# Row maxima of the values pinned behind the first two score maxima in a fused attention and MoE kernel

## Chip, cores and metric

The kernel runs on one core of one Trainium2 chip. The metric is the device time of one execution in microseconds (us). "Profile" and "trace" mean one execution recorded by the hardware profiler.

## What is computed

Two batches of eight heads, 768 positions, head size 64: attention in which a query sees only the keys of its own hash bucket (six sign bits of a projection), and then two dense layers over 1536 tokens.

```python
q_bits = (np.einsum('bhsd,dk->bhsk', q, proj) > 0)
mask = q_bucket[:, :, :, None] == k_bucket[:, :, None, :]
scores = np.where(mask, scale * np.matmul(q, k.transpose(0, 1, 3, 2)), -1000000000.0)
attn = np.exp(scores - np.max(scores, axis=-1, keepdims=True))
attn = attn / (np.sum(attn, axis=-1, keepdims=True) + 1e-09)
x = np.matmul(attn, v)          # then heads side by side: 1536 x 512
h = x @ w_in;  x = (h / (1 + exp(-h))) @ w_out
h = x @ w_in2; out = (h - tanh(h)) @ w_out2
```

## The kernel before

**Tiles.** A tile is 128 queries against the 768 keys of one head: 6 tiles a head, 48 a batch, numbered 0 to 95 here. For a tile `scores` (L243) makes four matmuls into PSUM tile `ps`. `soft_max` (L256, VectorE) copies them to `p` and takes their row maximum. `soft_exp` (L264, L265, ScalarE) takes the exponential. Then `p`, split into two float16 halves, is transposed into `pt`. Odd tiles of the first batch do that on TensorE (`turn_p`: L278, with L280 on ScalarE and L281 on VectorE). All others go through `soft_hi` (L290, ScalarE), `soft_lo` (L297, GpSimd) and a DMA transpose on SyncE's queue (L299). `pv` (L311 to L313) multiplies `pt` by the values; in the program it comes six tiles behind the scores.

**Hash bits.** `hash_mm(n)` (L172) runs once a head. VectorE turns its result into bits `hb` (L185), and two DMAs issued by ScalarE (L187, L188) copy them into the operands of the second half of the head's scores.

**Values.** `load_v` (L194) brings a batch's values into `vr` with three DMAs. `prep_vm` (L202, VectorE) takes the largest magnitude of each row, in six pieces of 128x512, into `vm`. `prep_v0` makes one scale `vsc` of them (L210 on VectorE, the matmul L212, L213 to L217 on VectorE). `prep_v2` splits the scaled values into `v16` (L232, ScalarE) and `v16l` (L233, VectorE), six pieces each; `pv` needs both. The second batch's `vr` lies in the same buffer as the first's, so its DMAs wait for the last L233 of the first batch.

**Stages.** The first batch's 48 tiles go with TensorE alone to themselves. From tile 33 on weights are loaded (L466) and split on VectorE (L507, L508, L510, L497), ScalarE (L498, L506) and GpSimd (L499). Thirteen steps pass without new scores between the batches. From tile 48 on scores have one `ps` buffer, not two, so a tile's scores wait for the maximum of the tile before. Groups of the first dense pass (L530, L554, twelve matmuls each) lie between the tiles of the second batch; the other passes follow after it.

**Order.** Every engine executes its own instructions strictly in a list order. The lists are made by a scheduler from the written program, from priorities and from its own estimate of time. `@early` (L92) raises the priority of what a function issues, so that the scheduler may place it ahead of older work. `tc.keep_in_program_order(...)` keeps an instruction in its place of the written order on its engine. In the loop over steps `prep_vm` is called behind `soft_exp` of a batch's first and second tile, three pieces each (L408).

Of the kernel before, what the change touches and what calls it, by code (L numbers as in the profile page):

```python
# [12 lines left out]
ALU = mybir.AluOpType  # L13
AXL = mybir.AxisListType
# [35 lines left out]
def lsh_attention_moe_kernel(  # L50
# [12 lines left out]
    nc = tc.nc  # L63
# [46 lines left out]
    def attention(pools, vraw, extra, xw):  # L110
# [9 lines left out]
        hlx, vmxs = {}, {}  # L120
# [70 lines left out]
        def load_v(b):  # L191
            vr = vraw.tile([128, NQ, DM], F32, tag="acc", name="vr")
            for t in range(0, NQ, 2):
                nc.sync.dma_start(out=vr[:, t:t + 2, :],  # L194
                                  in_=v[b, t * 128:(t + 2) * 128].rearrange("(t p) d -> p t d", p=128))
            return vr

        @early
        def prep_vm(b, vr, t):
            if t == 0:  # L200
                vmxs[b] = sm.tile([128, NQ], F32, tag="vm", name="vm")
            nc.vector.tensor_reduce(vmxs[b][:, t:t + 1], vr[:, t, :], axis=AXL.X, op=ALU.max,  # L202
                                    apply_absolute_value=True)

        @early
        def prep_v0(b, vr):
# [159 lines left out]
        vr = load_v(0)  # L366
# [8 lines left out]
        for s in range(B * (per + gap)):  # L375
# [18 lines left out]
            if i is not None:  # L394
                n, t = divmod(i, NQ)
# [9 lines left out]
            if i is not None:  # L405
                if i % per < 2:
                    for u in range(3):
                        prep_vm(n // H, vr, 3 * (i % per) + u)  # L408
                if i % per == 1:
                    prep_v0(n // H, vr)  # L410
                    prep_v1(n // H, vr)
                if 2 <= i % per < 4:
                    for u in range(3):
                        prep_v2(n // H, vr, 3 * (i % per - 2) + u)
                if prep[0] < NHEAD and prep[0] <= limit(n):
                    if prep[1] == 0:
                        split_a(prep[0])
                    elif prep[1] == 1:
                        split_b(prep[0])
                    prep[1] += 1  # L420
                    if prep[1] == 3:
                        prep[:] = [prep[0] + 1, 0]
                while nextr < NHEAD and nextr <= (limit(n) + 1 if n < H - 1 else n + (2 if t >= 3 else 1)):
                    load_qk(nextr)
                    nextr += 1
                if n + 1 < NHEAD:
                    if (n + 1) % H == 0 and t == 0:
                        vr = load_v((n + 1) // H)
# [304 lines left out]
```

## Time and profile before

| | |
|---|---|
| time, median of 3 runs | 792.09 us (791.6 to 792.28) |
| the profiled execution: its own time | 791.22 us |
| its span, first to last instruction | 789.4 us |
| TensorE busy (PE) | 733.6 us, 93% |
| VectorE (DVE) | 544.4 us, 69% |
| ScalarE (ACT) | 433.1 us, 55% |
| GpSimd (POOL) | 309.5 us, 39% |

The own time holds 1.8 us that lie around the span. PE's busy time is a sum over stages of very different kind; what an edit is worth is read from the stage in which it lies. PE in a row is TensorE's matmul, SPq and ACTq are the queues by which SyncE and ScalarE issue DMAs.

### The profile page before, as it was taken

Reading aid. Unit: us, or ns where it says so; the run is one execution under the profiler, and the core shown is the slowest. Engines: PE = TensorE matmul, PEld = TensorE weight load, DVE = VectorE, ACT = ScalarE, POOL = GpSimd, SP = SyncE. Lnnn points to the kernel's source line nnn. Section 1 sums busy time; section 2 is a strip of 40 time slices with the busy share of each in tenths; the row PEclk is TensorE's granted clock in tenths of the full one; section 3 lists DMA queues with packets and bytes.
Section 4 is the critical chain, followed back from the end, with each engine's and each line's share of the span. In section 5 each row is a group of like instructions: output and inputs, shape, how many; then the busy total and the mean of one; then the engine's idle time right before and its main releaser. Section 6 shows DMA issues by size and latency. Waiting matters only on the chain.

```text
span 789.4 us, 14334 instructions
## 1 busy us (share of the span) xinstructions
PE 733.6 (93%) x5492; PEld 700.0 (89%) x5492; DVE 544.4 (69%) x1029; ACT 433.1 (55%) x821; POOL 309.5 (39%) x214
## 2 busy tenths in 40 slices
PE   4778798789989899999999999999999999999998
PEld 3667677679978798899999999999999999999998
DVE  6968688798878778778542443998768576584342
ACT  4849788797788678667443441553524334242130
POOL 4536537466777667566455420222111110110000
PEclk8899899899999999999999999999999999999999
DMA  7695776969999899994333320323112121210102
GB/s 255 190 148 106 126 154 167 212 155 197 263 245 211 214 180 240 215 218 136 97 104 107 95 81 1 101 90 130 53 56 78 57 81 33 75 54 0 52 29 81
DMA packets 138879, 100.39 MB, mean 127 GB/s; under 512 B 115870, under 2 KB 118174, under 8 KB 138810
## 3 DMA queue, kind: packets, MB, share of 16 engines
q1 hardware_dynamic: 137712, 97.54, 50.6%
q10 hardware_dynamic: 1098, 1.94, 1.0%
q8 instruction: 43, 0.70, 0.3%
q14 instruction: 26, 0.21, 0.1%
HBM read 57.95 MB, written 11.53 MB: 88 GB/s over the span
## 4 chain that ended last, share of the span: by engine, by line
PE 55%; DMA 2%; ACT 1%; DVE 0%; issue 0%; POOL 0%; ACTq 0%; DVEq 0%
PE psm L554 28%; PE psm L530 26%; DMA pt<-hl 1%; DMA w<-wi 1%; PE ps L243 0%; ACT xh L577 0%; ACT p L265 0%; POOL hl L297 0%; PE pso L311 0%; POOL wl L485 0%; ACT wh L484 0%; ACT th L536 0%; PE pso L312 0%; PE pso L313 0%; ACT hl L290 0%
## 5 line engine op out<-in xcount | busy, mean ns | idle before, releaser
L499 POOL TENSOR_TENSOR wl<-wa,wh 128x512 fp32r<-128x512 f32 x64 | 83.8, 1309 | 244.3 <-ACT wh L498 244.3
L530 PE MATMUL psm<-xh,wh 128*128 128x384 f32 x512 | 173.2, 339 | 1.6 <-ACT wh L484 1.6
L554 PE MATMUL psm<-gh,wh 128*128 128x384 f32 x512 | 173.0, 338 | 0.6 <-ACT x L346 0.4
L554 PE MATMUL psm<-gl,wh 128*128 128x384 f32 x512 | 171.5, 335 | 0.0
L530 PE MATMUL psm<-xl,wh 128*128 128x384 f32 x512 | 171.4, 335 | 0.0
L530 PE MATMUL psm<-xh,wl 128*128 128x384 f32 x512 | 170.0, 335 | 0.0
L554 PE MATMUL psm<-gh,wl 128*128 128x384 f32 x512 | 169.4, 335 | 0.0
L297 POOL TENSOR_TENSOR hl<-p,hl 128x768 f16<-128x768 f32 x72 | 120.4, 1674 | 88.0 <-ACT hl L290 82.5
L256 DVE TENSOR_SCALAR_CACHE_REDUCE p<-ps 128x768 f32<-128x768 f32 x96 | 90.8, 952 | 29.7 <-PE ps L243 20.0
L530 PEld LDWEIGHTS psm<-xh,wh 128*128 128x128 f32 x512 | 96.5, 188 | 2.1 <-ACT wh L484 1.9
L243 PE MATMUL ps<-k,q 128*128 128x384 f32 x336 | 82.9, 372 | 15.9 <-DVE p L256 9.0
L554 PEld LDWEIGHTS psm<-gh,wh 128*128 128x128 f32 x512 | 96.3, 188 | 1.5 <-ACT x L346 0.6
L554 PEld LDWEIGHTS psm<-gl,wh 128*128 128x128 f32 x512 | 96.4, 188 | 0.0
L530 PEld LDWEIGHTS psm<-xl,wh 128*128 128x128 f32 x512 | 96.4, 188 | 0.0
L566 DVE TENSOR_TENSOR acc<-acc,psm 128x384 f32<-128x384 f32 x96 | 52.1, 551 | 63.5 <-PE psm L554 63.1
L530 PEld LDWEIGHTS psm<-xh,wl 128*128 128x128 f32 x512 | 95.9, 188 | 0.0
L554 PEld LDWEIGHTS psm<-gh,wl 128*128 128x128 f32 x512 | 95.8, 188 | 0.0
L542 DVE TENSOR_TENSOR gl<-psm,gh 128x384 fp32r<-128x384 f32 x128 | 70.6, 554 | 31.9 <-ACT gh L541 31.7
L265 ACT ACTIVATE p<-p,bi 128x768 f32<-128x768 f32 x96 | 89.0, 939 | 2.9
L541 ACT CAST gh<-psm 128x384 fp32r<-128x384 f32 x128 | 61.4, 480 | 50.5 <-DVE psm L540 35.1
L311 PE MATMUL pso<-v,pt 128*128 128x65 f16 x576 | 70.9, 200 | 15.4 <-DMA pt<-hl 15.3
L311 PEld LDWEIGHTS <-pt 128*128 128x128 f16 x576 | 55.3, 101 | 27.2 <-DMA pt<-hl 17.4
(90 smaller groups left out, 1267.2 us busy)
## 6 DMA issues: line engine op xcount, KB each, us to landing
w<-in_w_in_dram SPq DMA_DIRECT2D x32, 512.0 KB
w<-in_w_out_dram SPq DMA_DIRECT2D x32, 512.0 KB
r<-in_qkT_dram SPq DMA_DIRECT2D x15, 768.0 KB
wi<-wa SPq DMA_DIRECT2D x16, 256.0 KB
wo<-wa SPq DMA_DIRECT2D x16, 256.0 KB
w<-wi SPq DMA_DIRECT2D x16, 256.0 KB
w<-wo SPq DMA_DIRECT2D x16, 256.0 KB
vr<-in_v_dram SPq DMA_DIRECT2D x6, 512.0 KB
```

The costliest lines, as they stand in the source:

```text
L243: nc.tensor.matmul(out=ps[:, u, 0:HS], lhsT=a[:, t * 128:(t + 1) * 128], rhs=c[:, u * HS:(u + 1) * HS], start=(j == 0), stop=(j == 1))
L256: nc.vector.tensor_scalar(p.rearrange("p (c s) -> p c s", c=2), pss.pop(i)[:, :, 0:HS], FLOOR, None, op0=ALU.max, op1=ALU.max, accum_out=m)
L265: nc.scalar.activation(out=p, in_=p, func=ACTF.Exp, scale=0.125, bias=bi)
L297: nc.gpsimd.tensor_tensor(hl[:, 1, :], p, hl[:, 0, :], op=ALU.subtract)
L311: nc.tensor.matmul(out=o, lhsT=pt[:, kt, :], rhs=v16[:, kt, h, :], start=(kt == 0), stop=False)
L499: nc.gpsimd.tensor_tensor(ll, s, hh.bitcast(F32), op=ALU.subtract)
L530: nc.tensor.matmul(out=ps, lhsT=a[:, k, fs], rhs=b_[blk][:, k, :], start=(k == 0 and j == 0), stop=(k == KD - 1 and j == 2))
L541: nc.scalar.copy(gh[:, f, :], ps)
L542: nc.vector.tensor_tensor(gl[:, f, :], ps, gh[:, f, :].bitcast(F32), op=ALU.subtract)
L554: nc.tensor.matmul(out=ps, lhsT=a[:, f, ds], rhs=b_[:, f, :], start=(f == 0 and j == 0), stop=(f == F - 1 and j == 2))
L566: nc.vector.tensor_tensor(ac, ac, ps, op=ALU.add)
```

## The change

`prep_vm` loses `@early`, and its reduction is kept in program order.

```diff
-        @early
         def prep_vm(b, vr, t):
             if t == 0:
                 vmxs[b] = sm.tile([128, NQ], F32, tag="vm", name="vm")
-            nc.vector.tensor_reduce(vmxs[b][:, t:t + 1], vr[:, t, :], axis=AXL.X, op=ALU.max,
-                                    apply_absolute_value=True)
+            tc.keep_in_program_order(
+                nc.vector.tensor_reduce(vmxs[b][:, t:t + 1], vr[:, t, :], axis=AXL.X, op=ALU.max,
+                                        apply_absolute_value=True))
```

No instruction is added or removed in the computation; the scheduler's lists differ. VectorE's list at the start of the program (L179 and L181 write tile 0's hash bits, L202 are the row maxima, L256 the score maxima of tiles 0 to 3, L210 the first step to the scale):

```order
-L202 TENSOR_REDUCE vm<-vr 128x1 x2
 L179 TENSOR_SCALAR q_145<-psm,cst_sb 18x384
 L181 TENSOR_SCALAR k_147<-psm,cst_sb 18x384
-L202 TENSOR_REDUCE vm<-vr 128x1 x4
+L256 TENSOR_SCALAR p,mx<-ps 128x768
+L202 TENSOR_REDUCE vm<-vr 128x1 x3
+L256 TENSOR_SCALAR p,mx<-ps 128x768
+L202 TENSOR_REDUCE vm<-vr 128x1 x3
 L256 TENSOR_SCALAR p,mx<-ps 128x768 x2
 L210 TENSOR_REDUCE vmx<-vm 128x1
```

All six row maxima stood ahead of tile 0's score maximum; now three stand behind tile 0's and three behind tile 1's.

ScalarE's list somewhat later in the same opening (L187 and L188 are the two DMAs with head 1's hash bits, L232 the six pieces of `v16`, L280 the copies of tile 1's transposes):

```order
+L265 ACTIVATE p<-p,bi 128x768
+L187 DMA q_187<-hb 18x768
 L232 ACTIVATE v_221<-vr,vsc 128x8x64 x6
-L187 DMA q_187<-hb 18x768
+L280 CAST pt<-psm 128x384 x2
 L188 DMA k_189<-hb 18x768
```

The second DMA of the bits stood right behind the six pieces; now two copies more stand ahead of it, and the exponentials of tiles 4 and 5 (L265) stand ahead of the pieces, where there were those of tiles 0 to 3 alone.

TensorE's list in the first batch, near tile 27 (L172 with h and l makes the hash of head 5 in two groups of four, of which the second is shown here; L243 with 649 and 650 are scores of head 4, four matmuls a tile; L278 are transposes). Before:

```order
L243 MATMUL ps<-k_649,q_647 128x384 x2
L243 MATMUL ps<-k_650,q_648 128x384 x2
L172 MATMUL psm<-h_129,hw 82x384
L172 MATMUL psm<-l_130,hw 82x384 x2
L172 MATMUL psm<-h_129,hw 82x384
L278 MATMUL psm<-cst_sb,p 128x128 x3
```

And now:

```order
L172 MATMUL psm<-h_129,hw 82x384
L172 MATMUL psm<-l_130,hw 82x384 x2
L172 MATMUL psm<-h_129,hw 82x384
L243 MATMUL ps<-k_649,q_647 128x384 x2
L243 MATMUL ps<-k_650,q_648 128x384 x2
L243 MATMUL ps<-k_649,q_647 128x384 x2
L243 MATMUL ps<-k_650,q_648 128x384 x2
L278 MATMUL psm<-cst_sb,p 128x128 x9
L243 MATMUL ps<-k_649,q_647 128x384 x2
L243 MATMUL ps<-k_650,q_648 128x384 x2
```

Three tiles' scores that stood ahead of the end of this hash (the third is the one shown in the rows before) stand behind it now.

VectorE's list where the second batch begins. Before, from tile 48's score maximum (its batch's row maxima stand some forty tiles earlier in the list):

```order
L256 TENSOR_SCALAR p,mx<-ps 128x768
L281 TENSOR_TENSOR pt<-psm,pt 128x384 x2
L256 TENSOR_SCALAR p,mx<-ps 128x768
L319 TENSOR_SCALAR den<-pso,vsc 128x6
L320 RECIPROCAL den<-den 128x6
L329 TENSOR_TENSOR xt<-pso,den 128x6x64
L507 TENSOR_SCALAR cv<-cv 128x512
L256 TENSOR_SCALAR p,mx<-ps 128x768
L508 TENSOR_SCALAR cv<-cv 128x512
L213 TENSOR_REDUCE vmr<-psm 128x1
```

And now, from the same maximum:

```order
L256 TENSOR_SCALAR p,mx<-ps 128x768
L202 TENSOR_REDUCE vm<-vr 128x1 x3
L281 TENSOR_TENSOR pt<-psm,pt 128x384
L256 TENSOR_SCALAR p,mx<-ps 128x768
L507 TENSOR_SCALAR cv<-cv 128x512
L319 TENSOR_SCALAR den<-pso,vsc 128x6
L202 TENSOR_REDUCE vm<-vr 128x1 x3
L508 TENSOR_SCALAR cv<-cv 128x512
L320 RECIPROCAL den<-den 128x6
L256 TENSOR_SCALAR p,mx<-ps 128x768
L210 TENSOR_REDUCE vmx<-vm 128x1
L510 SCALAR_TENSOR_TENSOR cv<-w,cv 128x512
```

The six row maxima of the second batch, which stood near tiles 8 and 9 of the first, stand behind tiles 48 and 49. The last step to the scale (L217) stood between the maxima of tiles 51 and 52 and stands between those of 52 and 53 now.

## Rows read from the trace of the kernel before

**Rows 1.** Stages by windows: busy us of each engine, clock, DMA share, GB/s
```profile
0.00:46.00 46.00, 26.23 (x183) 21.94 (x184) 37.09 (x71) 30.00 (x51) 24.20 (x19) 0.89 0.79 214
46.00:134.00 88.00, 75.17 (x864) 64.73 (x861) 66.37 (x142) 68.68 (x136) 45.49 (x27) 0.92 0.66 132
...
152.00:182.00 30.00, 25.38 (x260) 23.55 (x259) 28.11 (x52) 25.99 (x49) 18.00 (x13) 0.95 0.68 173
182.00:362.00 180.00, 171.41 (x1584) 156.92 (x1582) 143.81 (x283) 135.98 (x243) 119.08 (x78) 0.99 1.02 218
362.00:789.40 427.40, 421.88 (x2433) 420.97 (x2432) 256.07 (x460) 160.08 (x323) 93.97 (x75) 1.00 0.22 70
```

**Rows 2.** Timeline of TensorE: start, us, work, idle before it and releaser
```profile
28.91 2.26 PE L243 MATMUL ps<-k,q 128*128 128x384 f32 x6 [3.27 <-DMA k<-hb]
...
45.47 0.20 PE L311 MATMUL pso<-v,pt 128*128 128x65 f16 x1 [3.43 <-DMA pt<-hl]
...
88.53 0.98 PE L243 MATMUL ps<-l,h 128*128 128x384 f32 x2 [3.45 <-DMA l<-hb]
```

**Rows 3.** What TensorE waited for, 134 to 400 us: total, times, longest
```profile
PE pso L311 <- DMA pt<-hl: 10.8, 7, 3.9
PE pso L312 <- DVE v16l L233: 3.6, 2, 2.2
```

**Rows 4.** Timeline of VectorE, opening
```profile
13.39 2.46 DVE L202 TENSOR_REDUCE vm<-vr 128x1 f32<-128x512 f32 x4
15.89 0.96 DVE L256 TENSOR_SCALAR_CACHE_REDUCE p<-ps 128x768 f32<-128x768 f32 x1
...
22.18 0.14 DVE L217 TENSOR_SCALAR vsc<-vmr 128x1 f32<-128x1 f32 x1
...
29.97 0.95 DVE L256 TENSOR_SCALAR_CACHE_REDUCE p<-ps 128x768 f32<-128x768 f32 x1
...
30.85 1.45 DVE L233 SCALAR_TENSOR_TENSOR v16l<-vr,vsc,v 128x512 f16<-128x512 f32 x1
```

**Rows 5.** ScalarE: the page's group of exponentials, then its timeline, opening
```profile
L265 ACT ACTIVATE p<-p,bi 128x768 f32<-128x768 f32 x96 | 89.0, 939 | 2.9
...
22.55 1.32 ACT L232 ACTIVATE v<-vr,vsc 128x512 f16<-128x512 f32 x2
...
24.89 0.74 ACTq L188 DMA_DIRECT2D k<-hb  x1
```

**Rows 6.** SyncE's queue: timeline in the opening, then the page's sizes of issues
```profile
32.32 1.41 SPq L194 DMA_DIRECT2D vr<-in_v_dram  x3
...
34.58 13.24 SPq L299 DMA_TRANSPOSE pt<-hl  x3
...
r<-in_qkT_dram SPq DMA_DIRECT2D x15, 768.0 KB
...
vr<-in_v_dram SPq DMA_DIRECT2D x6, 512.0 KB
```

**Rows 7.** Chain that ended last: one DMA transpose
```profile
322.84 5.53 DMA pt<-hl
```

**Rows 8.** Tiles vm and v16l on VectorE: ns min/median/max, starts
```profile
L202 DVE TENSOR_REDUCE vm<-vr x12: 675/676/687, 10.8 to 41.7; 128x1 f32<-128x512 f32 x12
L233 DVE SCALAR_TENSOR_TENSOR v16l<-vr,vsc,v x12: 740/776/2429, 23.3 to 176.6; 128x512 f16<-128x512 f32 x12
```

**Rows 9.** Timeline of VectorE where the second batch begins
```profile
152.27 0.95 DVE L256 TENSOR_SCALAR_CACHE_REDUCE p<-ps 128x768 f32<-128x768 f32 x1
...
164.22 0.15 DVE L217 TENSOR_SCALAR vsc<-vmr 128x1 f32<-128x1 f32 x1
...
172.02 2.43 DVE L233 SCALAR_TENSOR_TENSOR v16l<-vr,vsc,v 128x512 f16<-128x512 f32 x1
...
174.97 3.38 DVE L233 SCALAR_TENSOR_TENSOR v16l<-vr,vsc,v 128x512 f16<-128x512 f32 x2
```

**Rows 10.** Timeline of GpSimd, same place
```profile
171.83 2.07 POOL L159 TENSOR_TENSOR q<-r,q 64x768 fp32r<-64x768 f32 x1 [3.97 <-ACT q L151]
```

## Prediction

> **What bounds the kernel now.** I first cut the span into stages. In the windows [rows 1] read TensorE's busy time against the length of each. From 362 us on it is 421.9 of 427.4 us, from 182 to 362 us 171.4 of 180. Those stages end when TensorE has done its work, so whatever moves their beginning moves the end. Up to 46 us it is busy 26.2 of 46, and from 46 to 134 us 75.2 of 88: there TensorE stands because something else is late. The DMA share of 1.02 from 182 to 362 us says that the 16 DMA engines have work all that time too. An edit on VectorE counts by what it adds to or takes from TensorE's idle time before 362 us.
>
> So I read next, in TensorE's timeline, what ends its long waits [rows 2]. At 28.91 it has stood 3.27 us for head 1's hash bits (k<-hb). At 45.47 it has stood 3.43 us for the DMA transpose of tile 4. At 88.53 it has stood 3.45 us for head 5's hash bits. Where the second batch begins it stands 3.6 us in two pieces for `v16l` [rows 3]. The row maxima end none of these waits themselves. They are work in VectorE's list, and the question is what they push.
>
> **The opening.** Each row maximum takes 0.675 us [rows 8], 0.61 to 0.64 us from start to start (four in 2.46 us) [rows 4]. Before, two of them, from 10.8 on [rows 8], delay the second half of tile 0's bits by 1.3 us, and four more fill 13.39 to 15.85, so tile 0's maximum starts at 15.89. Take them away: the two operations on the bits end at about 12.1 instead of 13.4, I give the scores behind them 0.6 us, and tile 0's maximum starts at 12.7, 3.2 us earlier. That is the edit's gain, and it does not last. Tile 1's maximum waits for three row maxima: 12.7 + 0.9 + 1.9 = 15.5. Three more follow, and tiles 2 and 3 come at 18.2 and 19.1. In the new list tiles 4 and 5 come before the scale's steps (L213 on), so 18.2 + 4 x 0.9 = 21.8 is where these begin. They need 1.6 us up to 22.3 now; the new list puts a second eviction of hash bits (0.7 us) among them, and that one waits for hash matmuls which now stand behind the scores of tiles 4 and 5. The scale is ready at about 24.7 instead of 22.3.
>
> The loss grows on ScalarE. Its six pieces of `v16` began at 22.55, right behind the scale [rows 5]. In the new list five more items stand ahead of them (two copies for head 3, one half of tile 4, the exponentials of tiles 4 and 5), each at most as long as an exponential, 0.94 us [rows 5]; I count 0.85 each. What stands ahead of those five ends 0.8 us earlier by the opening above. So they begin at 22.55 - 0.8 + 4.25 = 26.0. The second hash DMA, issued at 24.89 and landed by 28.91, is behind two further copies of about 0.4 us: 24.9 + 3.45 + 0.7 = 29.0, landed at about 33. Tile 6's maximum, 29.97 now, comes at about 34.1, and behind it in VectorE's list are two pieces of `v16l` and tile 7's maximum (0.75, 0.9, 0.75), so the last L233 ends at 37.2 instead of 32.3. For that SyncE's queue waits: the second batch's `vr` is issued at 32.32 [rows 6], in its list ahead of tile 4's transpose, which is issued at 34.58 and lands at 45.47, 13.15 us behind `vr`'s issue. In the new list the 768 KB of `r` that stood between them go out earlier. One transpose alone takes 5.53 us [rows 7], which leaves 7.6 us for the 2304 KB ahead of it and 2.5 us for `r`, a third of them. Tile 4's transpose then lands at 37.2 + 13.15 - 2.5 = 47.9: **+2.4 us** at the point where, by both lists, TensorE has done the same work. What is queued behind is the whole of TensorE's list. Bounds: -2 (the `vr` DMAs no later and `r` out of the way) to +5 (the hash bits land at 36). The row maxima of the second batch no longer fill VectorE from 36 to 42 us; that saves TensorE nothing here, because the transpose of tile 4 lands later than they end.
>
> **The hash of head 5.** TensorE's new list has three tiles' scores behind this hash that stood ahead of its end. The 3.45 us wait at 88.53 then has twelve more matmuls beside it, of which two take 0.98 us there [rows 2], enough to cover it. But the bits' second DMA still waits on ScalarE behind a copy of transposes, which now stand behind two of those tiles. I take **-2 us**; bounds -3.4 (all of it) and 0.
>
> **The start of the second batch.** From tile 48's maximum at 152.27 to the end of the last `v16l` piece takes 26.1 us now [rows 9]. VectorE works in 28.1 of the 30 us around [rows 1], so there is little idle time in which six row maxima could hide. The new list adds between these two points six of them (3.7), L210 (0.15) and three steps of weight splitting (2.0), and leaves out two others (1.0): +4.8 us if the gaps stay. Two things counter it. The 1.9 us of gaps fill up. And the last three L233 took 2.43 and 3.38/2 us against 0.74 at best [rows 8, 9], while GpSimd subtracted operands of the next head [rows 10]; whether the later pieces meet that again the trace cannot tell. If none did, 4.0 us would be saved. So the last piece comes between 1.1 us earlier and 4.8 later. In TensorE's list one group of the dense pass (12 matmuls, 2.1 us) that lay ahead of the wait for it lies behind it now, which takes that cover away. Together -1.1 to +6.9; I take **+4**, nearer the upper end, because head 10's operands are prepared directly behind the scale in both lists and will meet these pieces again.
>
> The Trainium skill (page "SBUF — State Buffer", section "Who interferes with whom") says that a VectorE instruction with two SBUF inputs contends with a GpSimd instruction that reads SBUF, whichever comes first holding the shared ports to its end, and that a reduction does not. The trace agrees: L202 never leaves 675 to 687 ns, L233 ranges from 740 to 2429 [rows 8]. By that rule the moved row maxima cost their plain time anywhere, and each moved L233 may cost a whole GpSimd instruction; the third rival is that case.
>
> **After that.** From 182 to 362 us TensorE waits for transposes 6.9 us in all (10.8 [rows 3] less the 3.9 before). A later TensorE also shifts what feeds those DMAs, so I count no gain; bounds -4 to +3, because the lists there differ in many small places.
>
> **Sum.** +2.4 - 2 + 4 = +4.4 on the profiled execution's 791.2 us gives 795.6. The median of the runs is 0.9 above that execution, where it would be 796.5. I say **796**.
>
> **Rivals.**
> 1. *The gain stays and the losses are eaten.* Place: head 5's bits at 85 to 88.5 us. Its wait goes entirely (-3.4), while the lateness of 2.4 goes into the other waits between 46 and 134 us (12.8 us not busy [rows 1]) and the second batch's into the 6.9 us of waits for transposes. Time 791.2 - 3.4 = 788. For it: these waits exist. Against it: most are for things that TensorE's own work sets off. It decides if what is left of both losses is under 1.8 us. Chance 0.2.
> 2. *Nothing arrives at the end.* The DMA engines, busy all through 182 to 362 us [rows 1], set the pace of the second batch, and lateness of TensorE up to there is hidden behind them: 791 to 793. For it: the share of 1.02. Against it: TensorE is busy for 95% of that stage, which leaves 8.6 us to hide in. Chance 0.2.
> 3. *All six late pieces meet GpSimd.* 1.7 us each (2.43 - 0.74) makes 10.1 instead of 4.0 us, 6 us more: about 802. Chance 0.08.
>
> That the pin does nothing is excluded by VectorE's lists, in which all twelve reductions stand elsewhere. My forecast, a few us slower, has the rest, 0.52; its own range is 793.7 to 800.
>
> **Numbers.** 0.2% of 792 is 1.6 us, about what a measurement here can tell from no change. Slower: 0.52 + 0.08 = 0.6. Same 0.2, faster 0.2. The range 789.5 to 802 leaves out perhaps 0.12 below and 0.07 above.
>
> **What would show it.** Tile 0's maximum at 12 to 13 us, the scale at 24 to 25, k<-hb landing at 32 to 34, TensorE's wait for the first late transpose ending at 47 to 49. Head 5's wait of 1 to 2 us instead of 3.45. From tile 48's maximum to the last `v16l` piece 29 us or so, and TensorE waiting for `v16l` 6 us or more instead of 3.6. The end then follows the start of the dense passes unchanged. I would be wrong if the hash bits of head 1 landed by 30 us, if the pieces of `v16l` all took 0.75 us, or if scheduling differences between 182 and 362 us, which I have set to nothing, came to several us.

## Result and the profile after

The kernel became slower: a median of 799.46 us over four runs (797.97 to 802.77) against 791.85 us of the kernel before beside it; ratio 1.0111, 95% interval 1.0067 to 1.0156. The profiled execution took 797.97 us, its span 796.2.

The forecast of 796 named the right side and the size within 3.5 us. The trace shows that the time went elsewhere than I had said. These are the stages of the changed kernel by windows, as in [rows 1]:

```profile
0.00:46.00 46.00, 28.06 (x208) 23.26 (x209) 31.28 (x65) 30.96 (x53) 23.29 (x19) 0.89 0.71 214
46.00:134.00 88.00, 75.43 (x921) 66.69 (x919) 71.77 (x149) 75.55 (x148) 52.09 (x31) 0.94 0.73 153
152.00:182.00 30.00, 25.85 (x197) 24.32 (x198) 27.70 (x57) 25.68 (x48) 19.23 (x12) 0.90 0.73 164
182.00:362.00 180.00, 163.34 (x1531) 151.27 (x1531) 133.82 (x260) 128.82 (x225) 113.54 (x73) 0.98 0.98 213
362.00:796.20 434.20, 428.87 (x2461) 427.52 (x2457) 260.32 (x469) 163.87 (x331) 94.59 (x75) 0.99 0.23 69
```

TensorE is busier than before in the two stages up to 134 us and lacks 8.1 us in the stage from 182 to 362 us. The start of a tile's score maximum (L256) serves as a milestone, since all kernels have the same 96 tiles. Tile 12's starts at 51.44 us (55.80 before), tile 48's at 144.24 (152.27), tile 54's at 173.47 (179.21), tile 95's at 348.13 (350.00). So the lead is 4.4, 8.0, 5.7 and 1.9 us, and the span then ends 6.8 us later. **The first batch became 8 us faster, and everything behind it 14.8 us slower.**

TensorE's timeline, three waits of the first batch and two at the end of the second:

```profile
31.14 1.08 PE L243 MATMUL ps<-k,q 128*128 128x384 f32 x4 [1.45 <-DMA k<-hb]
...
44.15 0.20 PE L311 MATMUL pso<-v,pt 128*128 128x65 f16 x1 [1.53 <-DMA pt<-hl]
...
96.31 0.58 PE L243 MATMUL ps<-k,q 128*128 128x384 f32 x2 [0.67 <-DMA k<-hb]
...
361.48 0.20 PE L311 MATMUL pso<-v,pt 128*128 128x65 f16 x1 [3.49 <-DMA pt<-hl]
...
364.05 0.69 PE L530 MATMUL psm<-xh,wh 128*128 128x384 f32 x1 [1.84 <-DVE gl L542]
```

The two waits of the opening are shorter than in [rows 2], and the 3.45 us for head 5's bits have no successor: 0.67 us is the longest wait for hash bits between 80 and 100 us. What TensorE waited for from 134 to 400 us, as in [rows 3]:

```profile
PE pso L311 <- DMA pt<-hl: 19.7, 11, 3.5
...
PE pso L312 <- DVE v16l L233: 1.7, 1, 1.7
```

The wait for `v16l`, which I had expected to grow, halved. The wait for DMA transposes went from 10.8 to 19.7 us.

**The last 8.7 us** (a lead of 1.9 turned into 6.8 late) lie behind tile 95's maximum, and three things fill them. In TensorE's list 586 matmuls of the dense pass stand ahead of tile 95's scores where there were 600; 14 of them at 421.88/2433 = 0.173 us [rows 1] are 2.4 us. The waits behind it are 3.49 + 1.84 us; before they were 0.48 for a transpose, 0.39 and 1.57, so 2.9 more. And TensorE's granted clock fell behind these waits. The windows from 362 to 380 us, first the changed kernel:

```profile
362.00:380.00 18.00, 16.16 (x85) 0.81 0.24 74
```

and the kernel before:

```profile
362.00:380.00 18.00, 16.04 (x93) 1.00 0.40 120
```

16.16 x 0.19 makes 3.1 us. Together 8.4.

### The profile page after: what moved, and what is told of

It is laid out like the page before. It is cut to its first block, busy times and chain, and to the rows that moved or that the text cites. A ratio compares the mean times of both kernels' runs of the same rounds, so it can differ in the third digit from the quotient of the medians.

```text
span 796.2 us, 14335 instructions
## 1 busy us (share of the span) xinstructions
PE 735.8 (92%) x5492; PEld 704.9 (89%) x5492; DVE 539.8 (68%) x1029; ACT 434.9 (55%) x821; POOL 309.4 (39%) x214
## 4 chain that ended last, share of the span: by engine, by line
PE 61%; DMA 8%; ACT 2%; issue 2%; DVE 2%; POOL 2%; POOLq 0%; ACTq 0%; DVEq 0%
PE psm L554 30%; PE psm L530 28%; DMA pt<-hl 6%; PE ps L243 2%; DMA w<-in_w_in_dram 1%; DMA w<-wi 1%; POOL hl L297 1%; PE pso L311 0%; ACT hl L290 0%; ACT p L265 0%; PE psm L172 0%; PE pso L312 0%; DVE cv L508 0%; POOL wl L485 0%; PE pso L313 0%
## 5 line engine op out<-in xcount | busy, mean ns | idle before, releaser
L256 DVE TENSOR_SCALAR_CACHE_REDUCE p<-ps 128x768 f32<-128x768 f32 x96 | 90.4, 950 | 37.9 <-PE ps L243 27.3
L243 PE MATMUL ps<-k,q 128*128 128x384 f32 x336 | 84.4, 380 | 16.3 <-DVE p L256 12.8
L311 PE MATMUL pso<-v,pt 128*128 128x65 f16 x576 | 68.3, 197 | 26.6 <-DMA pt<-hl 24.6
L265 ACT ACTIVATE p<-p,bi 128x768 f32<-128x768 f32 x96 | 89.1, 937 | 3.2 <-ACT hl L290 0.2
```

The costliest lines, as they stand in the source:

```text
L243: nc.tensor.matmul(out=ps[:, u, 0:HS], lhsT=a[:, t * 128:(t + 1) * 128], rhs=c[:, u * HS:(u + 1) * HS], start=(j == 0), stop=(j == 1))
L256: nc.vector.tensor_scalar(p.rearrange("p (c s) -> p c s", c=2), pss.pop(i)[:, :, 0:HS], FLOOR, None, op0=ALU.max, op1=ALU.max, accum_out=m)
L265: nc.scalar.activation(out=p, in_=p, func=ACTF.Exp, scale=0.125, bias=bi)
L311: nc.tensor.matmul(out=o, lhsT=pt[:, kt, :], rhs=v16[:, kt, h, :], start=(kt == 0), stop=False)
```

## Experiments

The variants name the row maxima L201 instead of L202; other lines are those of the listing or shifted by one or two. Each time is a median; each ratio is to the kernel before on the same chip. The milestones come from one profiled execution each, and two executions of the change, with the same lists, differ by 3 us at tile 48, so smaller differences there say nothing; by the second of them the lead at tile 48 is 5.0 us instead of 8.0 and the loss behind it 17.2 instead of 14.8. A wait sum of one execution is no surer, as the kernels with tile 95 on TensorE show further down.

| kernel | tile 12 | tile 48 | tile 95 | waits for transposes, 182 to 362 us | time | ratio, 95% interval |
|---|---|---|---|---|---|---|
| before | 55.80 | 152.27 | 350.00 | 6.9 | 791.85, beside the others 790.12 to 792.16 | 1 |
| change | 51.44 | 144.24 | 348.13 | 14.4 | 799.46 | 1.0111, 1.0067 to 1.0156 |
| change, again | 52.39 | 147.32 | 352.73 | 12.9 | 799.9 | 1.0111, 1.0063 to 1.0159 |
| first batch only | 55.36 | 152.30 | 347.17 | 4.3 | 789.99 | 0.9969, 0.9933 to 1.0004 |
| second batch only | 48.89 | 142.29 | 354.07 | 8.9 | 799.82 | 1.01, 1.0054 to 1.0146 |
| pinned with raised priority | 52.00 | 144.57 | 346.73 | 5.5 | 792.08 | 1.0024, 0.9996 to 1.0053 |
| second batch's behind tiles 44, 45 | 53.52 | 152.95 | 351.72 | 9.1 | 792.54 | 1.0038, 1.0009 to 1.0068 |
| the same, first batch as before | 49.05 | 144.16 | 340.49 | 2.9 | 785.62 | 0.9936, 0.9909 to 0.9964 |
| the same, tiles 45, 46 | 47.96 | 147.66 | 349.24 | 11.3 | 795.49 | 1.0059, 1.0019 to 1.0099 |

**One batch at a time.** The theory of the prediction (the opening loses, the start of the second batch loses) against the one that the two traces suggest (the first batch gains, the second loses). In the edits `red()` issues the reduction, and `early` is the raised priority of `@early`.

```diff
-            tc.keep_in_program_order(red())
+            tc.keep_in_program_order(red()) if b == 0 else early(red)()
```

> Only the first batch's row maxima are pinned; the second batch's keep their raised priority, so only the opening of the lists differs from before and from about tile 20 on all lists are those of before. Prediction's theory: the opening loses 2.4 us, hence tile 48's maximum at 152 to 155 us (152.27 before) and the end at 793 to 795. Theory from the two traces: the pin in the opening is what gained, so hash 2's bits and tile 12 come 3 to 5 us earlier (tile 12's maximum at 51 to 53 instead of 55.80), tile 48's at 147 to 149, and since the lists of the second batch are unchanged most of it stays to the end: 786 to 789. Rival: the second batch is paced by its DMA engines and eats the lead: tile 48 earlier, end within 1.6 us of before.

With `b == 1` in place of `b == 0`:

> Only the second batch's row maxima are pinned, behind the maxima of tiles 48 and 49; the opening up to about 36 us is that of before. Prediction's theory: +4 at the start of the second batch, so 795 to 797, with v16l waits of 6 us or more. Theory from the two traces: the second batch with the pin loses about 10 to 15 us from tile 48's maximum to the end (637.1 us before, 652.0 with both pins), so the time is 797 to 806, unless VectorE freed at 36 to 42 us brings tile 48 forward by some us. Rival: the second batch's loss is no work of the pin but of lists that fall differently in many places; then this kernel's stretch from tile 48 to the end can lie anywhere from 632 to 652.

Both theories missed in the first of the two: 789.99 us, which its interval does not tell from before. Pinning the first batch does delay the opening, as the prediction said: tile 8's maximum comes 2.8 us later and tile 10's 3.5 us, but tile 12's hardly is (55.36 against 55.80, and 53.65 and 54.13 in two other executions of the order of before up to there), and tile 48's is the same. The pin of the second batch alone brings tile 12 forward by 6.9 us and tile 48 by 10.0. So the whole gain comes from **taking the second batch's row maxima out of VectorE's list at 36 to 42 us**, which I had priced at nothing. The timeline of VectorE with the first batch alone pinned shows what they do:

```profile
40.62 2.58 DVE L201 TENSOR_REDUCE vm<-vr 128x1 f32<-128x512 f32 x4 [1.01 <-DMA vr<-in_v_dram]
43.12 0.67 DVE L185 TENSOR_SCALAR hb<-psm,cst_sb 82x384 fp32r<-82x384 f32 x1
43.70 1.27 DVE L201 TENSOR_REDUCE vm<-vr 128x1 f32<-128x512 f32 x2
...
45.82 0.95 DVE L256 TENSOR_SCALAR_CACHE_REDUCE p<-ps 128x768 f32<-128x768 f32 x1
...
47.64 0.67 DVE L185 TENSOR_SCALAR hb<-psm,cst_sb 82x384 fp32r<-82x384 f32 x1
```

VectorE first waits for `vr`, then works 3.9 us on the row maxima, and the second half of head 2's bits comes behind them at 47.64. Without them, in the kernel with the second batch alone pinned, it comes at 40.51:

```profile
40.51 0.67 DVE L185 TENSOR_SCALAR hb<-psm,cst_sb 82x384 fp32r<-82x384 f32 x1
```

In the kernel before it comes at 44.64:

```profile
44.64 0.67 DVE L185 TENSOR_SCALAR hb<-psm,cst_sb 82x384 fp32r<-82x384 f32 x1
```

There the DMAs with these bits also stood in ScalarE's queue behind a copy of a transpose (L280) that TensorE makes only behind its 3.43 us wait of [rows 2]:

```profile
48.78 0.48 ACT L280 CAST pt<-psm 128x384 f16<-128x384 f32 x1 [4.25 <-PE psm L278]
48.90 0.76 ACTq L187 DMA_DIRECT2D h<-hb  x1
...
49.70 0.73 ACTq L188 DMA_DIRECT2D l<-hb  x1
```

and with the second batch alone pinned, ahead of that wait:

```profile
41.21 0.75 ACTq L187 DMA_DIRECT2D h<-hb  x1
...
42.00 0.73 ACTq L188 DMA_DIRECT2D l<-hb  x1
```

The bits leave 7.7 us earlier, 4.1 of them because VectorE writes the bits earlier and the rest by the DMAs' place on ScalarE's queue, and tile 12, the first of head 2, follows. The time of 799.82 agrees with the traces' theory, but does not yet say why the second batch loses; with 652.3 us from tile 48 to the end the rival is not excluded either.

**Is it the place behind tiles 48 and 49?** The same pins, the reduction issued with its raised priority besides. In the traces the arithmetic of every engine and SyncE's DMAs run in the change's order up to tile 49 (further than the forecast says), and in another order behind it. (No run here drops `@early` without the pin, so what that half of the change does by itself is not shown.)

```diff
-            tc.keep_in_program_order(red())
+            early(lambda: tc.keep_in_program_order(red()))()
```

> Both batches pinned as in the change, but the reduction keeps its raised priority; the lists are those of the change up to about tile 10 and fall differently behind it, with the row maxima behind tiles 48 and 49 as in the change. If the pinned place of the second batch's maxima is the cause of the loss, the stretch from tile 48's maximum to the end is again about 650 us, the time 797 to 801. If the loss is a matter of how the rest of the lists fell, the stretch differs by several us from 652.

792.08 us, 7 us less than the change, with the row maxima behind the same two tiles and tile 48 just as early. From tile 48's maximum to the end of the span it needs 789.0 - 144.6 = 644.4 us against 652.0 of the change and 637.1 of before. So the place itself is not the cause of the whole loss; 7.3 us of it are there in this kernel too.

**Another place.** Here the second batch's row maxima are written behind tiles of the first batch.

```diff
-                if i % per < 2:
+                if i < 46 and i % 44 < 2:
                     for u in range(3):
-                        prep_vm(n // H, vr, 3 * (i % per) + u)
+                        prep_vm(i // 44, vr, 3 * (i % 44) + u)
```

> Both pinned, but the second batch's row maxima are written behind tiles 44 and 45 of the first batch instead of behind tiles 48 and 49, so they neither fill VectorE at 36 to 42 us nor stand behind tile 48's maximum. If the pinned place at tiles 48 and 49 costs what was lost: tile 48 at 143 to 146, the last v16l piece about 26 us or less behind it, the stretch from tile 48 to the end near before's 637, and so 781 to 785. If the second batch does not take a lead over, wherever the maxima stand: tile 48 again 7 to 9 us earlier, but tile 95 at 346 to 351 as in all five kernels so far, and the time 788 to 796.

The second kernel also takes the pin from the first batch.

> As the run before (second batch's maxima pinned behind tiles 44 and 45), but the first batch's are left as before, so the opening's small losses are out. Tile 48 at 141 to 144 us. By the theory of the pinned place 779 to 783; by the theory that the second batch takes no lead over 786 to 798, tile 95 at 346 to 354.

792.54 and 785.62. The first has its last `v16l` piece 15.2 us behind tile 48's maximum, 12.6 us sooner than the change, and is still no faster than before, by its interval a little slower: its tile 48 comes 22 us behind tile 47 (18 before), and the shorter start of the second batch alone did not help. (In the traces of both kernels the second three maxima run behind tile 47, not 45.) The second is faster than both kernels of the study, with a time between the two ranges of its forecast. It keeps a lead of 8.1 us at tile 48 (9.5 at tile 95) to the end, which the theory that the second batch takes over no lead had excluded. What sets it apart is in the list of TensorE's waits from 182 to 362 us:

```profile
PE pso L311 <- DMA pt<-hl: 2.9, 3, 1.5
```

In the kernel before and in the change this row is

```profile
PE pso L311 <- DMA pt<-hl: 6.9, 6, 2.7
...
PE pso L311 <- DMA pt<-hl: 14.4, 9, 3.5
```

**Is its place what makes it fast?** The same kernel, one tile later (45 for 44).

> The fastest kernel so far with the second batch's row maxima one tile later, behind tiles 45 and 46 instead of 44 and 45; the lists agree up to about tile 43 and fall differently behind it. If the place of the row maxima makes that kernel fast: 784 to 788, tile 48's maximum at 142 to 146 and tile 95's at 340 to 344. If its 785.6 is how the lists of the second batch happened to fall: tile 48 is just as early, but the end lies anywhere from 788 to 800.

795.49: 1.25% apart by one tile. The row maxima run at 121.0 and 136.9 us where they ran at 117.7 and 139.3, tile 48 is early again, if by less, and the wait is back:

```profile
PE pso L311 <- DMA pt<-hl: 11.3, 7, 3.6
```

So the 785.6 is not the merit of the place alone, and the change's 799.5 not the fault of its own alone. The scheduler lays out the second batch anew after any shift, and the waits for transposes change with it: the change's order was executed three times, the third with tile 95 on TensorE, and waited 14.4, 12.9 and 12.3 us (in the second, another 3.87 us for the last transpose lie behind the window). Over the nine rows of the table the time follows that column nearly in order. The kernel with the second batch alone pinned stands out; it also waits 5.5 us for `v16l`. The five kernels below follow it less well: 3.0 us of waits at 790.32, 7.2 at 796.92, 12.3 at 797.13, 7.6 at 792.82 and 9.2 at 790.44. The order of the rows is a correlation; only the wait for the last tile was changed by itself.

**Does DMA volume eat the lead?** Each converted weight piece is written back (L501) with a quarter of its bytes.

```diff
-                nc.sync.dma_start(out=w, in_=dr)
+                nc.sync.dma_start(out=w.rearrange("p (a c) -> p a c", a=4),
+                                  in_=dr[:, None, 0:n // 4].to_broadcast([128, 4, n // 4]))
...
-                    nc.sync.dma_start(out=dr, in_=s)
+                    nc.sync.dma_start(out=dr[:, 0:w.shape[1] // 4], in_=s[:, 0:w.shape[1] // 4])
```

> The kernel before, with only a quarter of each converted weight piece written back to memory (64 instead of 256 KB; the later pass reads that quarter four times, so its weights are not the reference's). All engines' lists are those of before. If DMA volume paces the second batch, the waits for transposes between 182 and 362 us (6.9 us) fall to 2 or less and the time to 784 to 788. If it does not, they stay and the time is within 2 us of before.

> The change with the same lighter write-back (same part of the computation left out); its lists in the second batch differ from the change's in places. If DMA volume is what ate the lead, tile 48 is 8 us earlier as in the change and the lead now reaches the end: 777 to 783. If the pinned place or the fall of the lists is the cause, DMA relief gives the change no more than it gives the kernel before: 790 to 800.

790.32 (ratio 1.0002, 0.9969 to 1.0035) and 796.92 (1.0075, 1.0038 to 1.0111). The first keeps the order of the kernel before on every engine up to 378 us. The second leaves the change's order at tile 47, so it shows another fall of the lists besides the lighter pieces. The waits for transposes from 182 to 380 us came to 3.0 and 7.2 us. For the kernel before that is 3.9 us less, about what two executions of one order differ by further down, so that DMA volume makes its transposes late is likely and not shown. Both lighter kernels also have new waits behind 380 us, 3.6 and 3.3 us more TensorE idle time than before and the change have there (7.2 and 6.8 against 3.6 and 3.5). Less these, by a rough sum of medians and single traces, the relief would be worth 4.5 us to the kernel before (791.2 - 790.32 + 3.6) and 5.8 to the change (799.46 - 796.92 + 3.3). Between the two lighter kernels 6.6 us remain, so lighter pieces do not take away what sets the change apart.

**The last tile.** The change's longest wait is the transpose of tile 95. SyncE's queue there:

```profile
351.16 1.44 SPq L299 DMA_TRANSPOSE pt<-hl  x1
352.70 0.86 SPq L501 DMA_DIRECT2D wi<-wa  x1
353.66 0.39 SPq L466 DMA_DIRECT2D w<-in_w_out_dram  x1
354.14 2.22 SPq L299 DMA_TRANSPOSE pt<-hl  x1
```

A weight piece is written (L501) and another loaded (L466) between the last two transposes, and TensorE's wait for the last ends 7.3 us after its issue. Before, the two stood together:

```profile
351.86 4.47 SPq L299 DMA_TRANSPOSE pt<-hl  x2
```

The change again has the same order and waits 3.87 us for the last transpose. The lighter change has it too, with a quarter of the bytes written, and does not wait there at all; the kernels in which the two stand together wait 0 to 2.1 us. That the pieces in between make it late is argued from these rows; no run moved them alone. The edit makes tile 95 go through TensorE instead.

```diff
-            return i < H * NQ and i % 2 == 1
+            return i < H * NQ and i % 2 == 1 or i == 95
```

> The change, with the last tile alone (95) transposed on TensorE instead of by DMA; the lists are the change's word for word up to about that tile. In the change TensorE waits 3.49 us for that DMA transpose at 361.48, then 1.84 us for gl, and then runs at a granted clock of 0.53 for 5 us. If that one event holds nearly half of what is lost behind tile 48, the time falls by 4 to 6 us against the change, to 793 to 796, though the transposes add about 1.5 us of work to TensorE. If the loss lies spread over the second batch, the time stays within 2 us of the change.

> The kernel before with the same edit of the last tile; its lists are those of before up to there. Before, TensorE loses no more than 0.9 us around the last tiles, so by the first theory nothing is gained: 790 to 793. A gain of 4 us or more here would say that the edit helps whatever the lists, and that the run before says nothing on the change.

> The fastest kernel so far (second batch's row maxima pinned behind tiles 44 and 45, first batch's as before) with the last tile transposed on TensorE. Its trace shows no long wait for the last transposes, so 785 to 788, no gain; below 784 would say that the last tile costs there too.

> The change itself once more, beside the other three on the same chip, so that the first of them can be read against it: 798 to 800.

Against the change again (799.9), the change with this edit takes 797.13 us (ratio to before 1.0073, 1.0042 to 1.0104), 2.8 us less; the intervals of the two overlap, and I had expected 4 to 6. The kernel before with it takes 792.82 (1.003, 0.9997 to 1.0063) and the fastest kernel 790.44 (0.9998, 0.9961 to 1.0034), where 785 to 788 was expected. Most of that last difference cannot be the edit's. Up to tile 93 both kernels have, by their traces, one order on every engine, and yet that tile's maximum came at 340.09 instead of 331.84 us, behind 6.3 us of waits for transposes instead of 2.6; the longest, for the same transpose, took 4.4 us instead of 1.5:

```profile
PE pso L311 <- DMA pt<-hl: 9.2, 7, 4.4
```

So the same lists can wait several us more or less, and the 2.9 us of the fastest kernel is in part luck. What the edit does is read from tile 95's maximum to the end of the span. That stretch went from 448.1 us (448.9 in the change again) to 446.9 in the change, from 439.4 to 442.9 in the kernel before and from 441.0 to 442.8 in the fastest kernel. Where no long wait is to be saved the edit costs 1.8 to 3.5 us, and in the change it saves 1.2 to 2.0 beyond that. The windows from 340 to 380 us show that the event itself is gone; the change:

```profile
340.00:380.00 40.00, 34.67 (x272) 0.91 0.61 152
```

and with tile 95 on TensorE:

```profile
340.00:380.00 40.00, 37.01 (x299) 1.00 0.60 154
```

2.3 us more busy time and 34.67 x 0.09 = 3.1 us of clock: 5.4 us, the upper end of what the stretches give with the edit's cost added (3.0 to 5.5). So the last transpose is worth 3 to 5 us of the change's loss, by traces and, less surely, by times.

## Why the prediction was right, and where its steps were not

**The opening, +2.4: tile 12 came 4.4 us earlier instead.** The first half of the working held. VectorE's timeline after, in the opening and at the start of the second batch:

```profile
12.60 0.96 DVE L256 TENSOR_SCALAR_CACHE_REDUCE p<-ps 128x768 f32<-128x768 f32 x1 [0.53 <-PE ps L243]
...
25.78 0.15 DVE L217 TENSOR_SCALAR vsc<-vmr 128x1 f32<-128x1 f32 x1
...
31.76 0.96 DVE L256 TENSOR_SCALAR_CACHE_REDUCE p<-ps 128x768 f32<-128x768 f32 x1 [1.06 <-PE ps L243]
...
144.24 0.94 DVE L256 TENSOR_SCALAR_CACHE_REDUCE p<-ps 128x768 f32<-128x768 f32 x1
145.12 1.86 DVE L202 TENSOR_REDUCE vm<-vr 128x1 f32<-128x512 f32 x3
...
150.12 1.86 DVE L202 TENSOR_REDUCE vm<-vr 128x1 f32<-128x512 f32 x3
...
162.10 0.15 DVE L217 TENSOR_SCALAR vsc<-vmr 128x1 f32<-128x1 f32 x1
...
169.95 2.07 DVE L233 SCALAR_TENSOR_TENSOR v16l<-vr,vsc,v 128x512 f16<-128x512 f32 x3
```

Tile 0's maximum was put at 12.7 and came at 12.60; the scale at 24.7 and came at 25.8. Then "behind two further copies" failed: the second hash DMA left at 27.43, not at 29.0, and tile 6's maximum came at 31.76, not 34.1. ScalarE's timeline there:

```profile
27.21 0.72 ACT L232 ACTIVATE v<-vr,vsc 128x512 f16<-128x512 f32 x1 [1.12 <-DMA pt<-hl]
27.43 0.74 ACTq L188 DMA_DIRECT2D k<-hb  x1
27.84 3.16 ACT L232 ACTIVATE v<-vr,vsc 128x512 f16<-128x512 f32 x5
30.90 1.20 ACT L280 CAST pt<-psm 128x384 f16<-128x384 f32 x3
```

The DMA stands behind all six pieces and two of the copies in the list, and was issued when one piece had begun. SyncE's queue shows the next link:

```profile
34.96 1.41 SPq L194 DMA_DIRECT2D vr<-in_v_dram  x3
36.48 10.43 SPq L299 DMA_TRANSPOSE pt<-hl  x3
```

`vr` went 2.6 us later than in [rows 6] (I had said 4.9), and TensorE's wait for tile 4's transpose ended at 44.15 instead of 45.47. That freeing VectorE from 36 to 42 us "saves TensorE nothing here" is the step that failed most: it was worth 7 us at tile 12 (5.4 by the means of the three and four executions that share an order up to there) and 10 at tile 48, because head 2's bits, which I did not follow, wait in the same list. With that time already freed, the delay by the first batch's pin is near what I had said: tile 12 comes at 51.4 to 53.5 us in six executions with both batches pinned and at 48.0 to 50.6 in four with the second alone, 3.1 us apart in the mean. More can wait behind a stretch of a list than what the next long stall names.

**Head 5's hash, -2.** The wait went whole, -3.45 us, the lower bound, in a stretch where everything was early already.

**The start of the second batch, +4: the loss was there, at about half the size, and its parts were others.** The scale came 17.9 us behind tile 48's maximum (11.95 before), and the last `v16l` piece ended 27.8 us behind it: +1.7 us, where I took +2.9 and had bounds of -1.1 and +4.8 (the 4.0 us in the lower one add up to 3.6 by their rows, which makes it -0.7). The late L233 did not lose to GpSimd as I feared. The last three took 2.07 us together, and GpSimd's operation at the same time was the one that stretched, from 2.07 us [rows 10] to 3.96:

```profile
169.75 3.96 POOL L159 TENSOR_TENSOR q<-r,q 64x768 fp32r<-64x768 f32 x1 [3.38 <-issue]
```

The third rival had the opposite case. The Trainium skill (page "SBUF — State Buffer", section "Who interferes with whom") lets issue order decide which of the two blocks, so either outcome is possible by it. The rows agree that one engine lost and the other did not; which issued first they cannot tell, since by these records GpSimd's operation began 0.2 us ahead of VectorE's both before, where VectorE lost [rows 9] [rows 10], and after, where GpSimd did. The lead shrank by 2.3 us from tile 48 to tile 54, a little over half of what I took.

**182 to 362 us, 0, bounds -4 to +3: this carried the result.** I had written that I would be wrong if scheduling differences there came to several us. TensorE lacks 8.1 us of busy time in that stage, most of it waits for transposes, and the clock behind the last of them takes 3.1 us more. My first two rivals asked whether lateness would be hidden; there was earliness, and it was lost.

**The total** is right by luck, because two misses of opposite sign cancel: a first batch 8 us too pessimistic by my terms of +2.4 and -2, and a second batch about 11 us too optimistic by those of +4 and 0.

What stays open is which moves in the lists of the second batch make its transposes late. For the last tile the price of a late transpose is shown, and the order of weight pieces and transposes on SyncE's queue is only a likely cause; for the waits at 289, 301 and 328 us, which recur in both profiles of the change, no experiment here isolates the cause.

## What to carry to other kernels

When a scheduler places the work, an edit's own place is only a part of its price: compare the lists far behind it, and try a neighbouring place before you credit or blame the one you chose, since here one tile of shift moved the time by 1.25%. Follow every consumer that stands behind a removed or added stretch in its engine's list, not only those that the longest waits name. A lead in an early stage is worth what the waits of the later stages leave of it, so read first the end of the last stage in which the bound engine still waits. And execute the same lists twice before you build on a wait of one trace: here one wait took 1.5 and 4.4 us.

## What was not expected of the hardware

DMA issues on ScalarE's queue did not wait for the arithmetic ahead of them in the list to run, so "strictly in a list order" holds for the arithmetic alone: L188 left at 27.43 with five pieces of L232 and two copies L280 still to come, 3.5 us before the first of those copies began; before, at 24.89, with two pieces to come. An instruction ahead that itself waited for another engine held the DMA back (L280 at 48.78 behind a wait of 4.25 us for TensorE, and L187 at 48.90).

The granted clock fell to 0.53 from 365 to 370 us, close to the 1.2 GHz level, right behind waits of 3.49 and 1.84 us, with TensorE busy throughout:

```profile
365.00:370.00 5.00, 5.00 (x18) 0.53 0.47 157
```

18 matmuls were recorded in that window, and 31 in an equal one at full clock (375 to 380 us). So these waits were paid a second time in clock. The same came behind the wait of 4.4 us in the fastest kernel with tile 95 on TensorE (0.53 from 230 to 235 us), and not behind one of 2.25 us at 355 us in the kernel before with that edit (1.00 from 350 to 370 us).
